# Attention scores of a whole query group in one go, z of a batch in five pieces, logits dealt out anew

## The chip, the core and the metric

One core of a Trainium2 chip runs the program. The metric is device microseconds of one execution; the kernel before takes 2508.85 us, the median of 3 runs (2508.83 to 2512.48).

## What is computed

Attention over 8 batches of 2496 rows, and then a layer of 8 experts on its result. The first part, cut to what matters here:

```python
scores = (1.0 / S) * np.matmul(z, z.transpose(0, 2, 1))   # z: 8 x 2496 x 64
attn = np.maximum(scores, 0.0) ** 2
out = np.matmul(attn, v)                                   # v: 8 x 2496 x 256
x = u * out
logits = x.reshape(B * S, D) @ w_gate                      # 256 x 8
```

The second part sorts the logits, deals every expert the same number of rows and runs two matmuls per expert. The change doesn't touch it.

## The kernel before, in words

**Tiles.** A batch has KT = 20 key tiles of 128 rows (the last holds 64) and NQ = 5 query groups of 512 columns (the last holds 448). The list `seq` walks over batches, groups and key tiles: 800 steps, called n below. Group 0 of a batch begins at step n0, and a *window* below is the 20 steps of one group. g0 to g4 are the five windows of a batch.

**What a step does.** Every product of float32 is made from a high and a low half in float32r. `scores` (L1003 to L1017) makes the scores of two key tiles at a time, each with 64 rows of the PE array, so that two matmuls run side by side; three rounds (high·high, high·low, low·high) per pair. Each result, a PSUM tile `sc` of 128x512, is rectified and scaled into SBUF as `r` by `rectify` (L1019), on ACT (L1025) or "aside" on DVE (L1023). There are SCB = 6 tiles `sc`, in rotation, so the first tile of pair j waits for the release of tile 2j-6 and the second for that of tile 2j-5. Then ACT squares `r` in place (L1029), ACT or DVE makes the high half `hi` (`split_hi`, L1036 or L1038), DVE the low half `lo` (`split_lo`, L1047), and `av` multiplies with the halves of v: six matmuls of 128 rows (L1060, L1062, L1063) into two PSUM banks.

**Goes.** Scores aren't made step by step but GO = 10 key tiles at a time: a *go* is five pairs in a row. After the first 24 tiles (six goes of four) the goes begin at tile 24, 34, ... 794: 78 goes. A go runs LA = 4 steps before its first tile is used, so that four steps of `av` lie between the end of a go and the use of its first tile.

**Order.** From step 20 on the order on PE, ACT and DVE is the program's order, written out by hand. In a step n: the go that is due; what `first_in` holds; the squares and halves of step n+4; `av(n)`; what `todo` holds. So DVE has a go's asides first, and behind them the logits that were put at the same step.

**After a group.** At the end of a window `take_acc` copies the two banks to SBUF (DVE L1069 "the take", ACT L1071). PE turns them back two steps into the next window (`turn_back`, L1083), DVE multiplies with u (`post_mul`, L1094). Then follow 32 logits of the group: one DVE instruction over 128x256 for each of 4 row tiles and 8 experts (`post_logits`, L1111), which `logits_at` deals out: some with the go in the middle of the next window, some with the go that begins the window after it, some between. Only the logits of the batch's last row tile have 64 rows.

**z and v of the next batch.** `z_turn` transposes z of the next batch piece by piece (L955, two transposes), ACT and DVE split it (`z_whole`, L962 and L963), and eight DMAs on SP's queue put the halves into place. ZH and ZL are one tile of 2560 columns per batch, with two buffers. The five pieces of a batch are turned ten steps apart, over the windows g1 to g3. In g4 one v tile per step is split for the next batch (`split_v`, ACT L994, DVE L995). In g1 `settle` (some twelve short DVE instructions) finds the best expert of the previous batch's rows.

Of the kernel before, what the change touches and what calls it, by code (L numbers as in the profile page):

```python
# [8 lines left out]
F32 = mybir.dt.float32  # L9
F32R = mybir.dt.float32r  # L10
# [4 lines left out]
AF = mybir.ActivationFunctionType  # L15
# [838 lines left out]
def attention(tc, u, v, z, w_gate, xd, identf, made, first, scale):  # L854
    nc = tc.nc
    B, S, D = u.shape
    DQ = z.shape[-1]
    lg, m = first["lg"], first["m"]
    E = lg.shape[2]
    NT = S // 128  # L860
    TL = S - NT * 128
    KT = NT + 1
    DH = D // 128
    NQ = KT // 4
    J = B * NT + B // 2
    JP = lg.shape[1]
    LA = 4
    RING = KT + 2
    SCB = 6
    GO = KT // 2  # L870
    with ExitStack() as ctx:
        io = ctx.enter_context(tc.tile_pool(name="io", bufs=3))
        zp = ctx.enter_context(tc.tile_pool(name="zp", bufs=2))
# [42 lines left out]
            return src[b, :NT * 128].rearrange("(p i) d -> p i d", i=NT)  # L916

        def load(src, b, g, name, width, copies):
            t = io.tile([128, 4, width], F32, name=name, bufs=2 if width == DQ else 3)
            n = min(4, NT - 4 * g)  # L920
            nc.sync.dma_start(t[:, :n], rows(src, b)[:, 4 * g:4 * g + n])
            if n < 4:
                for c in range(copies):
                    nc.sync.dma_start(t[c * TL:(c + 1) * TL, n], src[b, NT * 128:])
            return t
# [14 lines left out]
            UR[b, g] = load(u, b, g, "ur", D, 2)  # L940

        def z_turn(b, g):
            if g == 0:
                ZH[b] = zp.tile([128, KT * 128], F32R, name="zh")
                ZL[b] = zp.tile([128, KT * 128], F32R, name="zl")
            p = ps.tile([128, 512], F32, name="sc", bufs=SCB)
            c = slice(512 * g, 512 * g + 512)
            t = ZI.pop((b, g))
            if (b, g) == (0, 0):
                for i in range(4):  # L950
                    nc.tensor.transpose(p[:, i * 128:i * 128 + 128], t[:, i].rearrange("p s d -> p (s d)"), identf)
                return (nc.scalar.activation(ZH[b][:, c], p, AF.Copy),
                        nc.vector.tensor_sub(ZL[b][:, c], p, ZH[b][:, c].bitcast(F32)))
            for i in range(2):
                nc.tensor.transpose(p[:, i * 128:i * 128 + 128],  # L955
                                    t[:, 2 * i:2 * i + 2].rearrange("p s d -> p (s d)"), identf)
            ZT[b, g] = p

        def z_whole(b, g):
            p = ZT.pop((b, g))[:, :256]  # L960
            h, l = [io.tile([128, 256], F32R, name=name, bufs=1) for name in ("zsh", "zsl")]
            nc.scalar.activation(h, p, AF.Copy)  # L962
            nc.vector.tensor_sub(l, p, h.bitcast(F32))  # L963
            for t, src in ((ZH, h), (ZL, l)):
                v4 = t[b][:, 512 * g:512 * g + 512].bitcast(F32).rearrange("p (i s q) -> p i s q", s=2, q=128)
                v3 = src.bitcast(F32).rearrange("p (i q) -> p i q", q=128)
                for s in range(2):
                    for half in range(2):
                        nc.sync.dma_start(v4[DQ * half:DQ * half + DQ, :, s], v3[DQ * s:DQ * s + DQ])

        def z_parts(b, g):
            c = slice(512 * g, 512 * g + 512)
            p = ZT.pop((b, g))
            zh, zl = [t[b][:, c].rearrange("p (i s q) -> p i s q", s=2, q=128) for t in (ZH, ZL)]
            src = p[:, :256].rearrange("p (i q) -> p i q", q=128)
            for s in range(2):
                r = slice(DQ * s, DQ * s + DQ)
                nc.scalar.activation(zh[r, :, s], src[r], AF.Copy)
            for s in range(2):
                r = slice(DQ * s, DQ * s + DQ)  # L980
                nc.vector.tensor_sub(zl[r, :, s], src[r], zh[r, :, s].bitcast(F32))

        def swap_z(b, c):
            for t in (ZH, ZL):
                v4 = t[b][:, c].bitcast(F32).rearrange("p (m s q) -> p m s q", s=2, q=128)
                nc.sync.dma_start(v4[:DQ, :, 1], v4[DQ:, :, 1])
                nc.sync.dma_start(v4[DQ:, :, 0], v4[:DQ, :, 0])

# [14 lines left out]
        def scores(lo, hi):  # L1003
            for n in range(lo, hi, 2):
                b, g, kt = seq[n]
                w = width(g)
                q = slice(g * 512, g * 512 + w)
                pair = [ps.tile([128, 512], F32, name="sc", bufs=SCB)[:, :w] for _ in range(2)]
                for key, query in ((ZH, ZH), (ZH, ZL), (ZL, ZH)):
                    for s in range(2):  # L1010
                        r = slice(DQ * s, DQ * s + DQ)
                        k = (kt + s) * 128
                        nc.tensor.matmul(pair[s], key[b][r, k:k + 128], query[b][r, q],  # L1013
                                         start=key is ZH and query is ZH, stop=key is ZL)
                for s in range(2):
                    SC[n + s] = pair[s]
                    rectify(n + s, n + s == lo + 1)  # L1017

        def rectify(n, aside):  # L1019
            p = SC.pop(n)  # L1020
# [9 lines left out]

        def split_hi(n):
            h = wk.tile([128, 512], F32R, name="hi", bufs=LA + 1)[:, :width(seq[n][1])]
            b, g, _ = seq[n]
            here = (0, 3, 5, 8) if g == NQ - 1 and b < B - 1 else (0, 4, 8)
            if n >= KT and ((n - LA) % GO not in here or n == B * NQ * KT - 2):
                nc.scalar.activation(h, R[n], AF.Copy)  # L1036
            else:
                nc.vector.tensor_copy(h, R[n])  # L1038
            HI[n] = h
# [148 lines left out]
        def at(n, f, *a):  # L1188
            todo.setdefault(n, []).append((f, a))

        def logits_at(m0):
            if m0 + KT < B * NQ * KT:
                g = m0 // KT - 1
                mid, more, end, rest = {NQ - 4: (14, 4, 14, 0), NQ - 3: (16, 6, 10, 0),
                                        NQ - 2: (8, 0, 14, 10)}.get(g % NQ, (14, 0, 14, 4))
                return ([m0 + GO] * mid + [m0 + GO + 3 + i for i in range(more)] + [m0 + KT] * end
                        + [m0 + KT + 4 + i % 6 for i in range(rest)])
            return [m0 + 4 + i // 2 for i in range(12)] + [m0 + GO] * 9 + [m0 + GO + 1 + i // 2 for i in range(11)]

        for c in range(0, (B - 1) * NT // 16 * 16, 16):  # L1200
            at((B * NQ - 1) * KT + 2 + c // 16, premask, c, c + 16)
        for b in range(B - 1):
            at(((b + 1) * NQ + 1) * KT + 12, settle, b * NT, (b + 1) * NT)
        for b in range(B):
            for g in range(NQ):
                n0 = (b * NQ + g) * KT
                m0 = n0 + KT
                if m0 == B * NQ * KT:
                    at(m0 - 6, turn_u, b, g)
                    at(m0 - 1, last_mul, b, g)  # L1210
                else:
                    for d in range(2):
                        at(m0 - 1, take_acc, b, g, d)
                    at(m0 + 2, turn_back, b, g)
                    for d in range(2):
                        at(m0 + 3, post_mul, b, g, d)
                for e, n in enumerate(logits_at(m0) if m0 < B * NQ * KT else ()):
                    first_in.setdefault(n, []).append((post_logits, (b, g, e // E, e % E)))
                if b or g:
                    at(n0 - 3, load_u, b, g)  # L1220
            n0 = b * NQ * KT
            if b == B - 1:
                at(B * NQ * KT + 1, last_logits, b, NQ - 1)
                at(B * NQ * KT + 2, settle, b * NT + 4 * (NQ - 1), J)
                at(B * NQ * KT + 3, last_rows, b, NQ - 1)
            if b:
                for g in range(NQ):
                    m = n0 + GO * (g - 2 * NQ + 2) + 5
                    at(m - 9, load_z, b, g)
                    at(m, z_turn, b, g)  # L1230
                    at(m + 1, z_whole, b, g)
                    at(n0 - KT + 4 * g - 8, load_v, b, g)
                for kt in range(KT):
                    at(n0 - KT + kt, split_v, b, kt)
            else:
                for kt in range(KT):
                    at(kt - 4, split_v, 0, kt)
                for g in range(1, NQ):
                    t = 4 * g - LA - 3
                    at(t, z_turn, 0, g)  # L1240
                    at(t + 1, z_parts, 0, g)
                    at(t + 2, swap_z, 0, slice(512 * g, 512 * g + 512))
                    if g >= 3:
                        at(4 * g - 13, load_z, 0, g)
                        at(4 * g - 11, load_v, 0, g)
# [70 lines left out]
```

## Time and profile before

| | |
|---|---|
| median of 3 runs | 2508.85 us |
| the profiled execution | 2515.77 us |
| its span, first to last instruction | 2514.0 us |
| granted TensorE clock, mean | 0.997 |
| attention, first to last score matmul | 5.9 to 1412.5 us |
| PE busy | 2472.2 us, 98% of the span |
| DVE busy | 2068.5 us, 82% |
| ACT busy | 1494.5 us, 59% |

The attention's 1.4 ms is the stretch that the change touches; the expert layer follows it. Matmuls are pipelined: a matmul of 512 columns has a duration of 0.39 us in the profile, and the next begins 0.23 us after it. So a change on PE is read from the distances between starts, not from busy time.

### The profile page before, as it was taken

The numbers are of one execution on the slowest core, as the hardware profiler recorded it, in microseconds if no ns is written. First come the engines' busy times: TensorE is split into PE (matmuls) and PEld (weight loads), VectorE is DVE, ScalarE is ACT, GpSimd is POOL, SyncE is SP. The second block draws the span as 40 slices with busy tenths as digits, with TensorE's granted clock in tenths as the row PEclk, the third lists the DMA queues.
The fourth block names the chain that finished last, engine by engine and source line by source line (L and its number), as shares of the span: only waits on it lengthen the run. The fifth ranks groups of instructions, "written<-read, shape, count | busy, mean of one in ns | idle before, by whom it ended". The sixth has DMA issues, their size and how long they took to land.

```text
span 2514.0 us, 43326 instructions
## 1 busy us (share of the span) xinstructions
PE 2472.2 (98%) x15350; PEld 2042.1 (81%) x15350; DVE 2068.5 (82%) x6370; ACT 1494.5 (59%) x2939; POOL 361.2 (14%) x508
## 2 busy tenths in 40 slices
PE   9999999999999999999999999999999999999997
PEld 6787888888888888878888878788888888888886
DVE  8888898898898898898888887979696969696332
ACT  7787887888787887878877522323232323233332
POOL 3000000000000000000000013233333333333332
PEclk9999999999999999999999999999999999999999
DMA  4222221221222112222110011212121212122110
GB/s 146 73 70 61 63 72 51 69 75 39 66 75 66 51 63 72 67 64 50 59 33 26 17 52 41 67 46 70 46 68 48 70 45 73 43 92 63 42 46 33
DMA packets 93721, 149.23 MB, mean 59 GB/s; under 512 B 16192, under 2 KB 61632, under 8 KB 93504
## 3 DMA queue, kind: packets, MB, share of 16 engines
q1 hardware_dynamic: 78272, 105.03, 14.2%
q0 software_dynamic: 15232, 41.44, 5.2%
q8 instruction: 120, 1.97, 0.3%
q14 instruction: 97, 0.79, 0.1%
HBM read 86.12 MB, written 40.89 MB: 51 GB/s over the span
## 4 chain that ended last, share of the span: by engine, by line
PE 88%; DVE 7%; issue 3%; ACT 1%; POOL 1%; DMA 0%; POOLq 0%; ACTq 0%; DVEq 0%; SPq 0%
PE acc L1060 14%; PE acc L1063 14%; PE acc L1062 13%; PE sc L1013 11%; PE y L748 10%; PE hp L652 5%; PE hp L653 5%; PE y L750 5%; PE hp L654 5%; PE srch L281 1%; PE sc L1083 1%; PE srch L529 1%; DVE mask L124 1%; DVE ob L523 1%; PE xp L325 1%
## 5 line engine op out<-in xcount | busy, mean ns | idle before, releaser
L1060 PE MATMUL acc<-hi,vh 128*128 128x512 f32 (+1 forms) x1600 | 631.7, 395 | 2.4 <-ACT vh L994 1.3
L1063 PE MATMUL acc<-hi,vl 128*128 128x512 f32 (+1 forms) x1600 | 616.2, 385 | 0.0
L1047 DVE TENSOR_TENSOR lo<-r,hi 128x512 fp32r<-128x512 f32 (+1 forms) x760 | 510.7, 677 | 117.1 <-ACT hi L1036 104.8
L1062 PE MATMUL acc<-lo,vh 128*128 128x512 f32 (+1 forms) x1520 | 586.4, 386 | 0.2 <-DVE lo L1047 0.2
L730 ACT ACTIVATE hh<-hp 128x512 fp32r<-128x512 f32 (+1 forms) x319 | 187.3, 587 | 592.0 <-PE hp L654 478.2
L1029 ACT ACTIVATE r<-r 128x512 f32<-128x512 f32 (+1 forms) x800 | 487.5, 651 | 1.7 <-DVE r L1023 1.5
L1111 DVE SCALAR_TENSOR_TENSOR lt<-xs,wgb 128x256 bf16<-128x256 f32 x1248 | 451.8, 421 | 1.0
L748 PE MATMUL y<-w,hh 128*128 128x512 f32 x1216 | 447.5, 400 | 2.4 <-DVE y L773 1.7
L1036 ACT ACTIVATE hi<-r 128x512 fp32r<-128x512 f32 (+1 forms) x533 | 342.9, 643 | 167.9 <-issue 111.9
L1025 ACT ACTIVATE r<-sc 128x512 f32<-128x512 f32 (+1 forms) x716 | 361.9, 609 | 94.4 <-PE sc L1013 87.6
L1060 PEld LDWEIGHTS acc<-hi,vh 128*128 128x128 f32 x1600 | 300.4, 188 | 83.2 <-issue 28.5
L1063 PEld LDWEIGHTS acc<-hi,vl 128*128 128x128 f32 x1600 | 300.3, 188 | 56.3
L1062 PEld LDWEIGHTS acc<-lo,vh 128*128 128x128 f32 x1520 | 285.7, 188 | 48.5 <-DVE lo L1047 0.5
L748 PEld LDWEIGHTS y<-w,hh 128*128 128x128 f32 x1216 | 228.2, 188 | 51.6 <-DVE y L773 3.0
L652 PE MATMUL hp<-xh,w1h 128*128 128x512 f32 (+2 forms) x642 | 256.7, 400 | 2.1 <-DVE hl__31174 L732 1.3
L590 POOL DMA_INDIRECT xg<-xd,idx x160 | 176.8, 1105 | 545.7 <-issue 245.1
L653 PE MATMUL hp<-xl,w1h 128*128 128x512 f32 (+2 forms) x642 | 251.0, 391 | 0.1
L654 PE MATMUL hp<-xh,w1l 128*128 128x512 f32 (+2 forms) x642 | 249.1, 388 | 0.0
L256 POOL IOTA slot<- 128x256 bf16 x1 | 1.5, 1532 | 1392.0 <-PE sc L1121 1392.0
L781 POOL DMA_INDIRECT out_dram<-y,idx x160 | 162.3, 1014 | 195.7 <-DVE y L773 111.1
L1013 PE MATMUL sc<-zh 64*128 64x512 f32 (+1 forms) x800 | 179.7, 416 | 4.9 <-DVE r L1023 4.2
L1013 PE MATMUL sc<-zl,zh 64*128 64x512 f32 (+1 forms) x800 | 169.6, 386 | 0.0
(1197 smaller groups left out, 3601.0 us busy)
## 6 DMA issues: line engine op xcount, KB each, us to landing
vr<-in_v_dram SPq DMA_DIRECT2D x32, 512.0 KB, 3.7
ur<-in_u_dram SPq DMA_DIRECT2D x32, 512.0 KB, 4.8
xd<-xs SPq DMA_DIRECT2D x32, 512.0 KB, 2.9
wr<-in_moe_w_dram SPq DMA_DIRECT2D x32, 512.0 KB, 5.4
zh<-zsh SPq DMA_DIRECT2D x140, 64.0 KB, 2.1
zl<-zsl SPq DMA_DIRECT2D x140, 64.0 KB, 2.0
zin<-in_z_dram SPq DMA_DIRECT2D x31, 128.0 KB, 2.2
vr<-in_v_dram SPq DMA_DIRECT2D x8, 384.0 KB, 3.3
```

The source lines that it names most:

```text
L652: nc.tensor.matmul(p[:, c], wh, xh, start=(d == 0), stop=False)
L653: nc.tensor.matmul(p[:, c], wh, xl, start=False, stop=False)
L654: latest["mm"] = nc.tensor.matmul(p[:, c], wl, xh, start=False, stop=(d == DH - 1))
L748: nc.tensor.matmul(o, h[:, c], w.rearrange("p s d -> p (s d)"), start=(f == 0), stop=(f == FT - 1), skip_group_check=True)
L1013: nc.tensor.matmul(pair[s], key[b][r, k:k + 128], query[b][r, q], start=key is ZH and query is ZH, stop=key is ZL)
L1025: recent["r"] = nc.scalar.activation(r, p, AF.Relu, scale=scale)
L1029: nc.scalar.activation(R[n], R[n], AF.Square)
L1047: recent["l"] = nc.vector.tensor_sub(l, a, h.bitcast(F32))
L1060: nc.tensor.matmul(o, vh, h, start=(kt == 0), stop=False)
L1062: nc.tensor.matmul(o, vh, l, start=False, stop=False)
L1063: nc.tensor.matmul(o, vl, h, start=False, stop=last)
L1111: nc.vector.scalar_tensor_tensor(t[r], XS[b, g][r, i], 1.0, WG["rows"][r, e], op0=OP.mult, op1=OP.mult, accum_out=lg[r, j, e:e + 1])
```

## The change

GO becomes 20: the goes begin at tile 24, 44, ... 784, 39 of them, one at the start of every window. Of a go's 20 tiles four (numbers 3, 6, 9 and 12) are rectified aside on DVE, where it was one of ten. DVE makes `hi` in five steps of a window (3 in 10 before, 4 in 10 in g4). Every batch has z in five pieces of 512 columns, and only piece 0 has two buffers; so pieces 1 to 4 of the next batch can be written only after the go that begins g4, and their turns move into g4 (steps 3, 7, 11 and 15), that of piece 0 to step 12 of g3. u has two buffers in place of three, `r` (whose count is GO + 3) 23 in place of 13. The logits: of most groups 18 between the steps of the next window and 14 with the go after it; those of g3 are dealt 6, 14 and 12, those of g4 12, 14 and 6, the last number standing for the window after that go. So DVE has these logits, before and after:

| window | before | after |
|---|---|---|
| g0 | 14 + 10 + 14 = 38 | 14 + 12 + 12 = 38 |
| g1 | 14 + 4 + 14 = 32 | 14 + 6 + 18 = 38 |
| g2 | 14 + 4 + 14 + 4 = 36 | 14 + 18 = 32 |
| g3 | 14 + 16 + 6 = 36 | 14 + 18 = 32 |
| g4 | 10 + 8 = 18 | 14 + 6 = 20 |

In the last window of all, `premask` of the first 128 rows' columns stands with the go instead of one call per step, and eight of the go's logits are moved ahead into the window before.

```diff
-    GO = KT // 2
+    GO = KT
+    HALF = GO // 2
+    ASIDE = (3, 6, 9, 12)
+    HERE = (2, 6, 10, 14, 18)
...
-            t = io.tile([128, 4, width], F32, name=name, bufs=2 if width == DQ else 3)
+            t = io.tile([128, 4, width], F32, name=name, bufs=3 if name == "vr" else 2)
...
         def z_turn(b, g):
-            if g == 0:
-                ZH[b] = zp.tile([128, KT * 128], F32R, name="zh")
-                ZL[b] = zp.tile([128, KT * 128], F32R, name="zl")
+            for part, name in ((ZH, "zh"), (ZL, "zl")):
+                part[b, g] = zp.tile([128, 512], F32R, name=f"{name}{g}", bufs=1 if g else 2)
...
                         r = slice(DQ * s, DQ * s + DQ)
-                        k = (kt + s) * 128
-                        nc.tensor.matmul(pair[s], key[b][r, k:k + 128], query[b][r, q],
+                        p, c = divmod(kt + s, 4)
+                        nc.tensor.matmul(pair[s], key[b, p][r, c * 128:c * 128 + 128], query[b, g][r, :w],
                                          start=key is ZH and query is ZH, stop=key is ZL)
                 for s in range(2):
                     SC[n + s] = pair[s]
-                    rectify(n + s, n + s == lo + 1)
+                    rectify(n + s, n + s == lo + 1 if hi - lo < HALF else n + s - lo in ASIDE)
...
         def split_hi(n):
-            b, g, _ = seq[n]
-            here = (0, 3, 5, 8) if g == NQ - 1 and b < B - 1 else (0, 4, 8)
-            if n >= KT and ((n - LA) % GO not in here or n == B * NQ * KT - 2):
+            if n >= KT and ((n - LA) % GO not in HERE or n == B * NQ * KT - 2):
...
         def logits_at(m0):
             if m0 + KT < B * NQ * KT:
-                g = m0 // KT - 1
-                mid, more, end, rest = {NQ - 4: (14, 4, 14, 0), NQ - 3: (16, 6, 10, 0),
-                                        NQ - 2: (8, 0, 14, 10)}.get(g % NQ, (14, 0, 14, 4))
-                return ([m0 + GO] * mid + [m0 + GO + 3 + i for i in range(more)] + [m0 + KT] * end
-                        + [m0 + KT + 4 + i % 6 for i in range(rest)])
-            return [m0 + 4 + i // 2 for i in range(12)] + [m0 + GO] * 9 + [m0 + GO + 1 + i // 2 for i in range(11)]
+                n = m0 // KT - 1
+                own, go, late = {NQ - 2: (6, 14, 12), NQ - 1: (12, 14, 6)}.get(n % NQ, (18, 14, 0))
+                if n == B * NQ - 3:
+                    own, go = own + go - 6, 6
+                return ([m0 + 4 + i * 16 // own for i in range(own)] + [m0 + KT] * go
+                        + [m0 + KT + 5 + i * 15 // max(late, 1) for i in range(late)])
+            return [m0 + 4 + i // 2 for i in range(4 * E)]
...
-            at((B * NQ - 1) * KT + 2 + c // 16, premask, c, c + 16)
+            first_in.setdefault((B * NQ - 1) * KT, []).append((premask, (c, c + 16)))
...
-                    m = n0 + GO * (g - 2 * NQ + 2) + 5
-                    at(m - 9, load_z, b, g)
+                    m = n0 - KT + (3, 7, 11, 15)[g - 1] if g else n0 -KT - 8
+                    at(m - 6, load_z, b, g)
                     at(m, z_turn, b, g)
                     at(m + 1, z_whole, b, g)
```

## Rows read from the trace of the kernel before

**Rows 1.** The page, part 1: busy time, share and instructions of each engine.

```profile
PE 2472.2 (98%) x15350; PEld 2042.1 (81%) x15350; DVE 2068.5 (82%) x6370; ACT 1494.5 (59%) x2939; POOL 361.2 (14%) x508
```

**Rows 2.** The waits, 100 to 1380 us: who waited for whom, us, times, longest.

```profile
PEld acc L1060 <- issue: 25.4, 72, 0.4
PEld sc L1013 <- issue: 25.1, 73, 0.4
...
PE sc L1013 <- DVE r L1023: 4.2, 7, 0.7
```

**Rows 3.** The timeline of PE around one go: start, us, instruction.

```profile
457.85 0.39 PE L1063 MATMUL acc<-hi,vl 128*128 128x512 f32 x1
458.17 0.50 PE L1013 MATMUL sc<-zh 64*128 64x512 f32 x2
...
458.97 0.39 PE L1013 MATMUL sc<-zh 64*128 64x512 f32 x2
...
460.79 0.41 PE L1013 MATMUL sc<-zh,zl 64*128 64x512 f32 x2
...
462.46 0.39 PE L1063 MATMUL acc<-hi,vl 128*128 128x512 f32 x1
```

**Rows 4.** Busy time by window: length, then PE, PEld, DVE, ACT, POOL, clock, DMA.

```profile
439.44:475.50 36.06, 36.06 (x191) 29.02 (x190) 31.83 (x106) 28.84 (x56) 0.00 (x0) 1.00 0.26 66
...
511.28:543.49 32.21, 32.21 (x187) 28.64 (x187) 29.17 (x86) 29.74 (x70) 0.00 (x0) 1.00 0.30 91
543.49:580.12 36.63, 36.00 (x188) 28.53 (x187) 32.94 (x113) 29.06 (x56) 0.00 (x0) 1.00 0.15 49
...
403.91:439.97 36.06, 36.06 (x192) 28.96 (x190) 32.92 (x111) 28.85 (x55) 0.00 (x0) 1.00 0.23 62
511.68:545.08 33.40, 33.40 (x200) 29.57 (x198) 30.33 (x89) 31.02 (x72) 0.00 (x0) 1.00 0.30 95
...
580.64:616.71 36.07, 36.07 (x192) 28.96 (x191) 32.21 (x111) 28.83 (x55) 0.00 (x0) 1.00 0.23 61
```

**Rows 5.** The timeline of DVE in one g1, whose go begins at 403.38.

```profile
404.51 0.68 DVE L1023 TENSOR_SCALAR r<-sc 128x512 f32<-128x512 f32 x1
405.11 0.42 DVE L1111 SCALAR_TENSOR_TENSOR lt<-xs,wgb 128x256 bf16<-128x256 f32 x1
...
410.18 0.43 DVE L1038 CAST hi<-r 128x512 fp32r<-128x512 f32 x1
...
412.24 0.69 DVE L1047 TENSOR_TENSOR lo<-r,hi 128x512 fp32r<-128x512 f32 x1 [0.30 <-ACT hi L1036]
...
423.14 0.69 DVE L1023 TENSOR_SCALAR r<-sc 128x512 f32<-128x512 f32 x1 [0.77 <-PE sc L1013]
...
439.36 0.69 DVE L1047 TENSOR_TENSOR lo<-r,hi 128x512 fp32r<-128x512 f32 x1 [0.55 <-ACT hi L1036]
```

**Rows 6.** The timeline of DVE in one g4 and at the go behind it.

```profile
516.89 0.40 DVE L1038 CAST hi<-r 128x448 fp32r<-128x448 f32 x1 [0.54 <-ACT r L1029]
...
536.61 0.63 DVE L1047 TENSOR_TENSOR lo<-r,hi 128x448 fp32r<-128x448 f32 x1 [0.28 <-ACT hi L1036]
...
545.08 0.62 DVE L1069 COPY at<-acc 128x448 f32<-128x448 f32 x1
...
545.95 0.68 DVE L1023 TENSOR_SCALAR r<-sc 128x512 f32<-128x512 f32 x1
```

**Rows 7.** The timeline of PE in the same go, which begins at 543.49.

```profile
545.67 0.39 PE L1013 MATMUL sc<-zh 64*128 64x512 f32 x1
546.69 0.50 PE L1013 MATMUL sc<-zh 64*128 64x512 f32 x1 [0.63 <-DVE r L1023]
```

**Rows 8.** The timeline of ACT in the go that begins at 403.38.

```profile
404.38 4.72 ACT L1025 ACTIVATE r<-sc 128x512 f32<-128x512 f32 x9 [0.63 <-PE sc L1013]
408.91 1.73 ACT L1029 ACTIVATE r<-r 128x512 f32<-128x512 f32 x3
```

**Rows 9.** The timeline of PE around one turn of z, which lies between these.

```profile
416.09 0.40 PE L1063 MATMUL acc<-hi,vl 128*128 128x512 f32 x1
...
417.01 0.39 PE L1063 MATMUL acc<-hi,vl 128*128 128x512 f32 x1
```

More of the change, by code (lines that the diff above doesn't have):

```diff
@@ L942, in z_turn @@
         def z_turn(b, g):
-            if g == 0:
-                ZH[b] = zp.tile([128, KT * 128], F32R, name="zh")
-                ZL[b] = zp.tile([128, KT * 128], F32R, name="zl")
+            for part, name in ((ZH, "zh"), (ZL, "zl")):
+                part[b, g] = zp.tile([128, 512], F32R, name=f"{name}{g}", bufs=1 if g else 2)
             p = ps.tile([128, 512], F32, name="sc", bufs=SCB)
-            c = slice(512 * g, 512 * g + 512)
             t = ZI.pop((b, g))
@@ L951, in z_turn @@
                     nc.tensor.transpose(p[:, i * 128:i * 128 + 128], t[:, i].rearrange("p s d -> p (s d)"), identf)
-                return (nc.scalar.activation(ZH[b][:, c], p, AF.Copy),
-                        nc.vector.tensor_sub(ZL[b][:, c], p, ZH[b][:, c].bitcast(F32)))
+                return (nc.scalar.activation(ZH[b, g], p, AF.Copy),
+                        nc.vector.tensor_sub(ZL[b, g], p, ZH[b, g].bitcast(F32)))
             for i in range(2):
@@ L964, in z_whole @@
             for t, src in ((ZH, h), (ZL, l)):
-                v4 = t[b][:, 512 * g:512 * g + 512].bitcast(F32).rearrange("p (i s q) -> p i s q", s=2, q=128)
+                v4 = t[b, g].bitcast(F32).rearrange("p (i s q) -> p i s q", s=2, q=128)
                 v3 = src.bitcast(F32).rearrange("p (i q) -> p i q", q=128)
@@ L971, in z_parts @@
         def z_parts(b, g):
-            c = slice(512 * g, 512 * g + 512)
             p = ZT.pop((b, g))
-            zh, zl = [t[b][:, c].rearrange("p (i s q) -> p i s q", s=2, q=128) for t in (ZH, ZL)]
+            zh, zl = [t[b, g].rearrange("p (i s q) -> p i s q", s=2, q=128) for t in (ZH, ZL)]
             src = p[:, :256].rearrange("p (i q) -> p i q", q=128)
@@ L981, in z_parts, with swap_z @@
                 nc.vector.tensor_sub(zl[r, :, s], src[r], zh[r, :, s].bitcast(F32))
-        def swap_z(b, c):
+        def swap_z(b, g):
             for t in (ZH, ZL):
-                v4 = t[b][:, c].bitcast(F32).rearrange("p (m s q) -> p m s q", s=2, q=128)
+                v4 = t[b, g].bitcast(F32).rearrange("p (m s q) -> p m s q", s=2, q=128)
                 nc.sync.dma_start(v4[:DQ, :, 1], v4[DQ:, :, 1])
@@ L1006, in scores @@
                 w = width(g)
-                q = slice(g * 512, g * 512 + w)
                 pair = [ps.tile([128, 512], F32, name="sc", bufs=SCB)[:, :w] for _ in range(2)]
@@ L1241, in attention @@
                     at(t + 1, z_parts, 0, g)
-                    at(t + 2, swap_z, 0, slice(512 * g, 512 * g + 512))
+                    at(t + 2, swap_z, 0, g)
                     if g >= 3:
```

## The prediction

> **What bounds the kernel now.** First the page: PE is busy for 98% of the span, DVE for 82%, ACT for 59% [rows 1]. Then the waits in the attention: PE almost never waits for another engine there; only seven times for an `r` of DVE, 4.2 us in all. But its weight loads stop for about 0.35 us in front of nearly every go and again in front of nearly every return to `av`, and nothing that the profile shows releases them [rows 2]. So the timeline of PE around a go: inside it the starts are 0.2275 us apart (eight starts in 460.79 - 458.97). From the last `av` before the go to the third after it are 18 starts; at that pace they would take 4.10 us, and they take 4.61 [rows 3]. **A go costs 0.51 us beside its matmuls.** Last the windows: 36.06 us for g2, 32.21 for g4, 36.63 for g0 [rows 4]. PE sets all of them, but in g0 something is added. A turn of z costs PE 0.24 (0.92 for three starts [rows 9], less 0.68), and g2 has two of them, g0 none: g0 ought to last 35.58 and is 1.05 longer. Rows 7 show why: in its first go pair 3 can start only its first matmul, and the second, which needs tile 1's buffer, comes 1.02 us later, released by DVE; there DVE's take starts at 545.08, 1.6 us after the go, and the aside ends at 546.63 [rows 6]. On time the take starts 0.53 us after the go (403.91 against 403.38 [rows 4, 5]).
>
> **What is removed.** 78 goes become 39: 39 x 0.51 = 19.9 us. The stall in g0 of seven batches, 7 x 1.05 = 7.3, goes too in its present form (tile 1 is no longer DVE's). Together 27.2 us, the most that the change can give. The turns of z stay five per batch, their DMAs eight per piece; only four come to lie in g4.
>
> **The go of 20 tiles on ACT.** The first pair is ready 1.00 us after the go begins (404.38 - 403.38), each later one 3 x 0.2275 = 0.68 after the one before; ACT takes a tile every 0.503 ((408.91 - 404.38) / 9), the last of nine lasting 0.70 [rows 8]. Pair 3 starts at 2.18 [rows 7], pair 5 at 3.54, pair 9 at 6.28; a release reaches PE 0.06 after the end of the instruction (546.69 - 546.63). Sixteen tiles are ACT's. Tile 5, the fifth, is free at 1.00 + 4 x 0.503 + 0.70 + 0.06 = 3.77, 0.23 after pair 5 wants it; tile 13, the tenth, at 6.29, in time. No go before has this order. The ends are 0 (the goes of ten show no stall of this kind beyond their 0.51) and 0.23; I take the middle, 0.1. Where a window is set by DVE (next part) such a stall gives DVE as much time, so it counts in the other 25 of 39: 2.5 us.
>
> **The go on DVE.** Asides stand ahead of the logits, and DVE takes its instructions in order: in the second go of g1 it waits 0.77 us with 14 logits behind [rows 5]. Tiles 3, 6, 9 and 12 belong to pairs 1, 3, 4 and 6, ready at 1.68, 3.05, 3.73 and 5.10. A rectify takes 0.60 (405.11 - 404.51). So DVE waits 0.55, 0.77, 0.08 and 0.77 us: 2.2 in a go where it is on time, and 2.0 in g4 by the same sum with 448 columns. In exchange its waits for ACT's `hi` behind a go come half as often; I leave one of 0.30 per window [rows 5].
>
> **DVE in g1.** It is busy for 32.92 us of 36.06 where the previous batch is an odd one, and its six listed waits (0.30 first, 0.55 last) make 2.49 [rows 4, 5]; the 0.65 left is gaps that count as occupied, 33.57 in all. The change adds two rectifies (1.20) and six logits at 0.36 ((410.18 - 405.11) / 14), 2.16; it takes away one cast (0.43) and two z subtractions, priced as logits, of the same 128x256 (0.72). That is 35.8, with the waits 2.2 and 0.3 **38.3 us**. PE needs 36.06 - 0.51 - 2 x 0.24 = 35.1. DVE comes 3.2 late to the go of g2. Where the previous batch is even it is busy 0.71 less [rows 4] and 2.5 late. What that costs PE: tile 3 is free 0.53 + 0.60 + 0.69 + 0.06 = 1.88 us after the go plus the lateness, and pair 4 wants its buffer at 2.86. So 0.98 is free, and PE stalls 2.2 (three batches) or 1.5 (four): 3 x 2.2 + 4 x 1.5 = **12.6 us**. The first batch has neither the six late logits nor a `settle` here.
>
> **DVE in g4.** From take to take it takes 33.40, with waits of 2.72 (six, 0.54 first and 0.28 last [rows 6]): 30.7 occupied. Two rectifies of 448 columns (0.60 x 448/512 = 0.53 each) add 1.05, two logits 0.72, four z subtractions 1.44; three casts less save 1.15. With waits of 2.0 and 0.3 that is 35.0 us. PE needs 32.21 - 0.51 + 4 x 0.24 = 32.7 [rows 4]. DVE is 2.3 late at the go of g0. There 0.87 lie between take and rectify (a v split stands between [rows 6]), so 0.7 is free and PE stalls 1.6: 7 x 1.6 = **11.2 us**. In g2 and g3 DVE has four logits fewer than before and fits; in g0 it has as many, two rectifies more, one cast less, and the go's stall gives it the time.
>
> **What costs nothing.** ACT loses two rectifies per window and gains one `hi` (three in g4). u's two buffers: a load waits for a product that is done 14 steps earlier. z's pieces are written behind the last go that reads the old ones; the last is split in step 16 of g4, and its first reader is pair 6 of the next go, three steps and six pairs later; load_z, the eight copies and load_v keep their order on SP. `premask` and 32 logits fall into a last window that has no v to split. Without that cover a late piece would stall PE in the go of g0, where it waits for DVE anyway.
>
> **Sum.** 27.2 - 2.5 - 12.6 - 11.2 = 0.9 us gained. The profiled execution's 2515.77 becomes 2514.9; it lies 6.9 above the median of the runs, and I carry the difference over: **2508 us**. A measurement of this kernel tells some 0.2%, 5 us, from no change.
>
> **Rivals.** (1) *DVE keeps up.* The lateness is a small difference of large sums, and a window's 38.3 against 35.1 would be undone by 3 us of error: if the waits in the go overlap the lateness, or DVE starts g1 and g4 ahead. For it: the goes are seldom stalled today, with DVE at 32 of 36 us. Against: its reserve there is 3 us, and 3 us of work and waits are added to g1. Then 27.2 less up to 4 for the goes is left, 2482 to 2486; with half of the lateness the stalls come to some 6.5, and 2491 is left. Chance 0.25.
>
> (2) *The goes are paced by their evacuation, and the kernel is slower.* Place: the six `sc` buffers. PE finishes a tile every 0.34 us, ACT needs 0.503, and 16 x 0.503 = 8.05 us of copies face 30 x 0.2275 = 6.83 of matmuls. Only the last six tiles may be left over, and tile 13 comes out just in time above; ACT's reserve is the 0.63 it idles before a go [rows 8]. If every go loses 0.5 more than figured, 25 x 0.5 = 12.5 us are lost: 2520. It decides from 0.2 per go on. For it: no go so far is longer than five pairs. Against: ACT idles 7 us in most windows [rows 4]. Chance 0.18. The Trainium skill has a rule that speaks for this one (TensorEngine Tiling (Array Packing), PSUM Bottleneck): tiling makes TensorE faster but not the emptying of PSUM, whose copies may become the bottleneck; ScalarE and VectorE should share them. By the rule the longer of the two, 8.05, would set the go, 1.2 us more in each of 39, some 48 us; by the rows only what the six buffers can't hold counts, so next to nothing.
>
> (3) *ACT comes last in g4.* It is busy 31.02 of 33.40 there [rows 4]; one more tile at some 0.44 and four z copies at no more than that make 32.9, beside 0.6 of waiting at the go, and PE's time on the same count is 33.9. If ACT is 2.3 late, it adds 0.7 to DVE's 1.6, seven times: 2513. Chance 0.12.
>
> **How the numbers follow.** The forecast has 0.45: 2501 to 2514, of which 0.13 lie under 2503.8 and 0.03 over 2513.9. Faster: 0.13 + 0.25 = 0.38. Slower: 0.03 + 0.18 + 0.04 of (3) = 0.25. Within 0.2%: 0.37. The range, 2487 to 2520, leaves out the best of (1) and the worst of (2).
>
> **What would show it.** 39 goes of 30 starts, a window of g2 or g3 at some 35.1 to 35.2 us; PE waiting for DVE's `r` in the go of g0 and of g2, by 1 to 2 us each, and nowhere else; DVE waiting three or four times in a go. If the go of g2 shows no stall, the account of g1 is wrong; if g2 and g3 are longer than 35.5, the go is; if ACT has no idle time in front of g0's go, (3) holds.

## The result and the profile after

The changed kernel takes **2544.09 us** (median of four runs, 2539.55 to 2546.16) against 2509.21 us of the kernel before (four runs): a ratio of **1.0134, interval [1.0116, 1.0151]**. It is slower, where no change was forecast. The profiled execution took 2546.16 us, with a span of 2544.1. One execution of run 2 below was in a slow state (4869 us) and is left out of its ratio.

The page's first part after, to be held against [rows 1]: the busy times of PE, DVE and ACT have hardly moved, and PE's share has fallen.

```profile
PE 2474.9 (97%) x15350; PEld 2069.9 (81%) x15350; DVE 2093.8 (82%) x6395; ACT 1489.7 (59%) x2914; POOL 361.5 (14%) x508
```

Windows after, from go to go, as in [rows 4]: g4 of batch 1 (batches count from 0), then g0 to g3 of batch 2, and last a stretch inside that g4. The columns are the stretch, its length, then busy time and count of PE, PEld, DVE, ACT and POOL, TensorE's granted clock, the DMA engines' share and GB/s.

```profile
338.29:376.30 38.01, 34.58 (x196) 30.90 (x195) 29.16 (x87) 31.68 (x76) 0.00 (x0) 0.96 0.39 93
376.30:413.17 36.87, 35.68 (x188) 28.88 (x188) 35.35 (x119) 28.43 (x54) 0.00 (x0) 1.00 0.33 104
413.17:448.37 35.20, 35.20 (x187) 29.34 (x186) 32.61 (x111) 27.97 (x53) 0.00 (x0) 1.00 0.09 31
448.37:485.26 36.89, 35.48 (x187) 28.68 (x187) 33.24 (x106) 28.11 (x53) 0.00 (x0) 1.00 0.09 29
485.26:520.52 35.26, 35.26 (x189) 29.34 (x189) 30.91 (x98) 27.72 (x54) 0.00 (x0) 1.00 0.18 50
...
371.00:374.40 3.40, 3.40 (x11) 3.00 (x10) 0.48 (x1) 1.60 (x4) 0.00 (x0) 0.53 0.41 82
```

In the batch shown g0 to g3 are within half a microsecond of the prediction's working. **g4 is not:** 38.01 us where PE needs 32.7, and PE is not even busy in it (34.58 of 38.01). The seven windows of this kind take 37.56 to 39.93 us, 38.14 on average: 5.4 us too long each, 38 us in all seven.

Who waits, from the waits after, 100 to 1380 us (us in all, times, longest us); [rows 2] are the same view before:

```profile
PEld sc L956 <- DMA zin<-in_z_dram: 27.6, 14, 4.6
PE sc L956 <- DMA zin<-in_z_dram: 23.5, 11, 4.2
ACT zsh L963 <- DMA zh<-zsh: 32.1, 13, 3.9
DVE zsl L964 <- DMA zl<-zsl: 24.3, 11, 4.8
PE sc L1012 <- DVE r L1022: 9.2, 9, 1.5
PEld acc L1057 <- issue: 12.1, 35, 0.4
PEld sc L1012 <- issue: 9.9, 28, 0.4
```

The last two lines are the gain that was forecast: the stops of the weight loads that nothing shown releases have halved or more, at the return (25.4 us in 72 before) and ahead of a go (25.1 us in 73). The first four are new, and all belong to z's pieces: PE waits for the load of a piece, ACT and DVE wait until the copies out of the single staging tiles `zsh` and `zsl` have landed. What stands behind these loads and copies is shown by SP's queue in that g4 (start, length and count of the issues):

```profile
351.28 0.33 SPq L924 DMA_DIRECT2D zin<-in_z_dram  x1
352.70 1.25 SPq L970 DMA_DIRECT2D zh<-zsh  x2
354.04 0.54 SPq L1095 DMA_DIRECT2D xd<-xs  x1
354.63 1.27 SPq L970 DMA_DIRECT2D zh<-zsh  x2
356.00 2.54 SPq L970 DMA_DIRECT2D zl<-zsl  x4
358.59 0.59 SPq L924 DMA_DIRECT2D vr<-in_v_dram  x1
359.28 2.54 SPq L970 DMA_DIRECT2D zh<-zsh  x4
361.93 2.85 SPq L970 DMA_DIRECT2D zl<-zsl  x4
364.84 0.58 SPq L924 DMA_DIRECT2D vr<-in_v_dram  x1
365.47 1.16 SPq L927 DMA_DIRECT2D vr<-in_v_dram  x2
366.73 0.53 SPq L924 DMA_DIRECT2D zin<-in_z_dram  x1
367.31 1.10 SPq L927 DMA_DIRECT2D zin<-in_z_dram  x2
368.51 2.62 SPq L970 DMA_DIRECT2D zh<-zsh  x4
371.22 3.22 SPq L970 DMA_DIRECT2D zl<-zsl  x4
374.49 0.59 SPq L924 DMA_DIRECT2D ur<-in_u_dram  x1
375.18 2.55 SPq L970 DMA_DIRECT2D zh<-zsh  x4
```

From 352.70 on SP issues with hardly a pause to the end of the window. A copy takes it 0.605 us (median of 280), a piece has eight, 4.84 us, and with the loads of v, u and z between them it needs more: from the first copy of one piece to that of the next (352.70, 359.28, 368.51, 375.18) pass 6.6, 9.2 and 6.7 us. PE turns a piece every four steps, 5.1 us. So the pieces fall behind, and the load of the last one, which the code puts six steps ahead of its turn, is issued only at 366.73, behind the copies of the second piece. PE's last product of `av` stands at 365.93; the turn waits:

```profile
365.93 0.36 PE L1060 MATMUL acc<-hi,vl 128*128 128x448 f32 x1
369.49 0.33 PE L956 MATMUL sc<-identf,zin 128*128 128x128 f32 x1 [3.20 <-DMA zin<-in_z_dram]
370.05 0.30 PE L956 MATMUL sc<-identf,zin 128*128 128x128 f32 x1 [0.23 <-DMA zin<-in_z_dram]
...
371.98 0.57 PE L1059 MATMUL acc<-lo,vh 128*128 128x448 f32 x1
372.35 0.57 PE L1060 MATMUL acc<-hi,vl 128*128 128x448 f32 x1
```

Idle time is not all: after it the products start 0.37 us apart instead of 0.20, from 371.23 to 374.59, and the granted clock of 371.00 to 374.40 is 0.53: nearly all of it at 1.2 GHz, the lower of TensorE's two levels. Until 365.93 PE had been busy at the full clock (2.4 GHz), then it stood idle, and it had run again for 1.7 us when the clock fell. Nine starts at 0.37 for 0.20 are 1.5 us. With 3.4 us of waiting that makes 4.9 of the 5.3 us that this window lost.

### The profile page after: what moved, and what is told of

Same layout as the page of the kernel before. It is cut to its first block, busy times and chain, and to the rows that moved or that the text cites. A ratio compares the mean times of both kernels' runs of the same rounds, so it can differ in the third digit from the quotient of the medians.

```text
span 2544.1 us, 43329 instructions
## 1 busy us (share of the span) xinstructions
PE 2474.9 (97%) x15350; PEld 2069.9 (81%) x15350; DVE 2093.8 (82%) x6395; ACT 1489.7 (59%) x2914; POOL 361.5 (14%) x508
## 5 line engine op out<-in xcount | busy, mean ns | idle before, releaser
L1033 ACT ACTIVATE hi<-r 128x512 fp32r<-128x512 f32 (+1 forms) x586 | 372.1, 635 | 211.9 <-issue 147.4
L1108 DVE SCALAR_TENSOR_TENSOR lt<-xs,wgb 128x256 bf16<-128x256 f32 x1248 | 475.2, 419 | 2.2
L1024 ACT ACTIVATE r<-sc 128x512 f32<-128x512 f32 (+1 forms) x638 | 313.9, 613 | 46.5 <-PE sc L1012 45.7
L1012 PE MATMUL sc<-zh,zl 64*128 64x512 f32 (+1 forms) x800 | 197.4, 386 | 0.5 <-DMA zl<-zsl 0.4
L1012 PE MATMUL sc<-zl,zh 64*128 64x512 f32 (+1 forms) x800 | 197.1, 387 | 0.0
```

The costliest lines, as they stand in the source:

```text
L1012: nc.tensor.matmul(pair[s], key[b, p][r, c * 128:c * 128 + 128], query[b, g][r, :w], start=key is ZH and query is ZH, stop=key is ZL)
L1108: nc.vector.scalar_tensor_tensor(t[r], XS[b, g][r, i], 1.0, WG["rows"][r, e], op0=OP.mult, op1=OP.mult, accum_out=lg[r, j, e:e + 1])
```

## The experiments

Ratios are to the kernel before, timed beside it on the same chip (its medians were 2509 to 2517 us). The trace of a run is of one execution. In the expectations A is the theory that z's crowded place in g4 costs the time, B one that does without it, and D the rival that holds the DMA engines' load responsible. The later ones say what they mean by S and T.

**1. Only z's place, in the kernel before.** Goes of ten, z in one tile, logits as they were.

```
-                    m = n0 + GO * (g - 2 * NQ + 2) + 5
-                    at(m - 9, load_z, b, g)
+                    m = n0 - KT + (3, 7, 11, 15)[g - 1] if g else n0 - KT - 8
+                    at(m - 6, load_z, b, g)
```

> The kernel before (goes of 10, z with two buffers) with one edit: the turns and loads of z stand where the change puts them (piece 0 in g3, pieces 1 to 4 in g4 at steps 3, 7, 11 and 15). Theory A (SP issues the eight z copies of a piece in 8 x 0.605 = 4.8 us, with the loads some 6 us per piece, while PE gives it only 5.1 us between two turns in g4): the loss comes with the place of the turns alone, 2535 to 2550 us, PE waiting for zin in g4 and the clock at half behind it. Theory B (the go of 20 tiles, or the evacuation, makes it slow): no loss here, 2507 to 2513.

Measured: 2560.64 us, 1.0176 [1.0159, 1.0193], 43 us over before and above A's range. The move alone costs more than the whole change: z's crowded place is enough for a loss of this size, and the rest of the change is worth something. But the loss falls in another place than A had it. No turn waits for `zin`; most of it is in the first ten-tile half of g0, which takes 22.3 to 25.6 us in place of 19.5. There PE waits for ACT's `r` (13.1 us in all, seven times), while ACT and DVE wait for the staging tiles (24.3 and 19.2 us).

**2. The loads of z earlier** (four buffers of `zin`; to make room, one of `r` less).

```
-                    at(m - 6, load_z, b, g)
+                    at(n0 - 2 * KT + 4 * g, load_z, b, g)
```

> The changed kernel with the five loads of z moved ahead into g2 and g3 (four zin buffers; r has one buffer less, 22, to make room). Theory A (SP's issue time for the copies is the bound): PE no longer waits for zin, but the copies still follow one another at some 5 us per piece, so ACT and DVE wait for zsh and zsl and the last pieces land at the go of g0: only a part comes back, 2515 to 2532. Theory C (only the load of the last piece stands too late in SP's order): the whole loss of 5.4 us per g4 comes back, 2544 - 38 = 2506, at most 2510.

Measured: 1.0087 [1.0067, 1.0107]. The wait for `zin` is gone and g4 takes some 32.7 to 33.8 us, but the go behind it lasts 11.7 to 16 us in place of 7.6: the wait has moved on, to the split of the last piece: in the go of g0 PE waits in every batch for the `sc` tile that DVE's `zsl` frees (7.9 us in all). By the ratios some 12 us came back, by the attention's own time (the table below run 12) 6.7.

**3. The copies of zl on POOL's queue.**

```
-                        nc.sync.dma_start(v4[DQ * half:DQ * half + DQ, :, s], v3[DQ * s:DQ * s + DQ])
+                        (nc.sync if t is ZH else nc.gpsimd).dma_start(v4[DQ * half:DQ * half + DQ, :, s], v3[DQ * s:DQ * s + DQ])
```

> The changed kernel with the four copies of zl of each piece issued by POOL in place of SP, which halves SP's work per piece to about 2.4 us and leaves transfers and order alone. Theory A: no wait for zin, g4 windows of 32.7 to 33.5 in place of 38.1, 2503 to 2510; if one POOL issue takes over 1.3 us the stalls stay in part. Theory D (the DMA engines are too busy in g4, their share is 0.7 there): the copies land as late as before, 2538 to 2546.

Measured: 1.0142 [1.0125, 1.0159], no gain. The wait for `zin` is all but gone (1.9 us in place of 23.5) and g4 takes 34.1 to 36.0 us, but the go of g0 now lasts 12 to 17.6: DVE waits 34.5 us in all for the staging tile, and PE 25.6 for DVE's `r` and 12.9 for `zsl`. So A was right on the turns and wrong on the time. The total alone would speak against SP's queue as a cause; runs 9 to 11 show why it had to miss.

**4. The same, with the logits of g0 dealt out anew** (fewer at the go of g2).

```
-                own, go, late = {NQ - 2: (6, 14, 12), NQ - 1: (12, 14, 6)}.get(n % NQ, (18, 14, 0))
+                own, go, late = {NQ - 2: (6, 14, 12), NQ - 1: (12, 14, 6), 0: (12, 14, 6)}.get(n % NQ, (18, 14, 0))
```

> As the run with zl on POOL, and besides the logits of g0 dealt 12, 14 and 6 in place of 18, 14 and 0, so that g1 has 32 and g2 38 of them. My account of DVE in g1 says the stall in the go of g2 (1.8 us in three batches, 0.4 in four) goes: 7 us less than the run with zl on POOL. If that stall has another cause (the 64-row logits, settle), no more than 2 us less.

Measured: 1.0138 [1.0121, 1.0155]. The windows of g2 fell to 35.2 us, so the stall there was DVE's. The medians differ by 3.2 us only, where the executions of run 3 alone differ by 6.5. Run 8 repeats it on better ground.

**5. Four DMAs per piece and no staging tile** (ACT and DVE write the halves in place, with twice the instructions).

```
-                    at(m + 1, z_whole, b, g)
+                    at(m + 1, z_parts, b, g)
+                    at(m + 2, swap_z, b, g)
```

> The changed kernel with z split straight into its pieces by ACT and DVE (two instructions each in place of one, as the first batch does it) and only the other half copied: 4 DMAs per piece in place of 8, and no staging tiles zsh and zsl. Theory A2 (a piece takes too long through one staging tile and eight issues one after the other on SP: zsh and zsl are free again only when their copies are issued and have landed): g4 falls from 38.1 to 33 to 34 us (ACT has 4 x 0.27 and DVE 4 x 0.34 us more there), 0.5 to 0.9% faster than the changed kernel. Theory D (the DMA engines are too busy): half the copies are gone too, so it gains some as well, but the loads of zin still come late. If neither, no more than 0.2%.

Measured: 1.0045 [1.0028, 1.0061], 0.9% under the changed kernel. g4 comes down to 32.7 to 33.2, while the go of g0 still lasts 10 to 13.4 us: there PE now waits for DVE's `r` (14.7 us in all). DVE has the extra instructions; that they make it late is likely, and was not tested by itself.

**6. Two buffers of each staging tile** (one of `r` less).

```
-            h, l = [io.tile([128, 256], F32R, name=name, bufs=1) for name in ("zsh", "zsl")]
+            h, l = [io.tile([128, 256], F32R, name=name, bufs=2) for name in ("zsh", "zsl")]
```

> The changed kernel with two buffers for zsh and zsl (r has 22 in place of 23). If the single staging tile is what spaces the pieces, ACT and DVE no longer wait for copies, and a third or more of the loss comes back (10 us and up). If SP's issue time of 4.8 us per piece is, next to nothing changes, since the copies only queue up later: within 5 us of the changed kernel.

Measured: 1.0094 [1.0077, 1.0111]. Now g0 takes 35.2 to 35.6 in six of seven batches, nearly without a stall (39.6 in the seventh), and g4 still 36 to 39: the turns wait for `zin` (22.4 us in all) behind SP's copies.

**7. Three pieces with two buffers, turned early; only two in g4** (one step of the ring, two buffers of `r` and the buffer of `ztwo` pay for it).

```
-                part[b, g] = zp.tile([128, 512], F32R, name=f"{name}{g}", bufs=1 if g else 2)
+                part[b, g] = zp.tile([128, 512], F32R, name=f"{name}{g}", bufs=1 if g > 2 else 2)
...
-                    m = n0 - KT + (3, 7, 11, 15)[g - 1] if g else n0 -KT - 8
-                    at(m - 6, load_z, b, g)
+                    m = n0 - KT + (4, 12)[g - 3] if g > 2 else n0 - KT - (32, 20, 8)[g]
+                    at(m - 9, load_z, b, g)
```

> The changed kernel with two buffers for z's pieces 0 to 2, turned in g3 and before (32, 20 and 8 steps before g4 ends its predecessor), and only pieces 3 and 4 in g4, at steps 4 and 12, 8 steps apart (11 us per piece). Room comes from r (21), the v ring (21) and the first z tile. Theory A: two pieces of 16 copies fit between their turns, g4 is 32.7 to 33.5 us, the stall of g0 at most 1.5: 34 us less than the changed kernel, that is -0.1% to -0.5% of the kernel before. If the go of 20 tiles itself is what costs, still over 1% slower than before.

Measured: 2501.73 us, **0.9942 [0.9925, 0.9958]**, faster than before. Its windows of g4 and the g0 behind it:

```profile
331.08:363.26 32.18, 32.18 (x191) 29.32 (x190) 30.30 (x92) 30.98 (x74) 0.00 (x0) 1.00 0.40 104
363.26:398.62 35.36, 35.36 (x187) 28.67 (x186) 33.44 (x112) 28.43 (x54) 0.00 (x0) 1.00 0.24 76
```

PE is busy in the whole of both. Copies and staging tiles are as in the changed kernel; the distance between the pieces is another, and with it the loads stand nine steps ahead of the turns in place of six.

**8. Run 7 with the logits of run 4.**

> As the run before it, with the logits of g0 dealt 12, 14 and 6. The stall in the go of g2 (1.8 us in three batches, 0.4 in four) goes: 6 to 8 us less than the run before it, 0.4 to 0.8% faster than the kernel before.

Measured: 2495.06 us, **0.9912 [0.9895, 0.9929]**, 6.7 us under run 7. g2 is at 35.4 in every batch but the last (35.2), where it was 35.4 to 35.8 in some and 37.2 in the others.

Runs 2, 3 and 6 each mended one thing and got back little or nothing. So they were put together.

**9. Runs 2 and 6 together** (early loads, two staging buffers).

> The changed kernel with both one-edit repairs together: the loads of z's pieces one go earlier (four buffers of zin) and two buffers of each staging tile zsh and zsl. Each alone gave back something (ratios to before 1.0087 and 1.0094). Theory S (SP's issue time of the copies is a bound by itself: eight at about 0.6 us, at least 5 us per piece beside the other loads, against 5.1 us between two turns): the pieces stay crowded on SP, and the last one is late; g4 and the go of g0 together still hold at least 3 us more per batch than in e7_z_two (32.2 and 35.4), so a ratio of 1.000 to 1.006. Theory T (the late load and the single staging tile are all of it): g4 32 to 33, the following g0 at most 36, so a ratio of 0.994 to 0.997.

Measured: 2523.91 us, 1.0059 [1.0042, 1.0076], as S has it. No load of z is late and no staging tile is awaited, yet the go of g0 lasts 10 to 13 us. Two of its waits (all batches together) and one of its matmuls, in a go that began at 367.81; then what SP had still to issue, with DVE's end of the last split:

```profile
PEld sc L1012 <- DMA zl<-zsl: 13.8, 12, 1.8
PE sc L1012 <- DMA zl<-zsl: 9.8, 7, 1.5
```

```profile
376.12 0.49 PE L1012 MATMUL sc<-zh,zl 64*128 64x512 f32 x1 [1.43 <-DMA zl<-zsl]
```

```profile
364.09 2.62 SPq L970 DMA_DIRECT2D zh<-zsh  x4
365.46 0.42 DVE L964 TENSOR_TENSOR zsl<-sc,zsh 128x256 fp32r<-128x256 f32 x1
366.82 2.54 SPq L970 DMA_DIRECT2D zl<-zsl  x4
369.45 2.55 SPq L970 DMA_DIRECT2D zh<-zsh  x4
372.10 2.54 SPq L970 DMA_DIRECT2D zl<-zsl  x4
```

DVE has finished the last piece's `zsl` at 365.88, ahead of the go, and SP issues the copies of the last two pieces back to back until 374.64, 6.8 us into it. The first product that needs the last copy runs at 376.12.

**10. Run 9 with the copies of zl on POOL** (the edit of run 3).

> e9_zin_staging with the copies of zl issued by POOL instead of SP, so that SP has four copies per piece (2.4 us) instead of eight. Theory S: most of what e9 still loses comes back: g4 and the following g0 within 1.5 us of e7_z_two's, a ratio of 0.994 to 0.999. Rival D (what holds the pieces is the landing of the copies on DMA engines that are loaded anyway, not their issue): no better than e9 within 0.2%.

Measured: 2495.97 us, **0.9946 [0.9929, 0.9962]**: the same edit that gave nothing in run 3 is worth 28 us, 1.1%, here (20.6 of them in the attention), and all five pieces stay where the change put them. Windows of g4 and g0, which answer to the first two shown above:

```profile
330.94:363.56 32.62, 32.62 (x195) 29.71 (x194) 30.80 (x93) 31.58 (x76) 8.46 (x15) 1.00 0.53 132
363.56:400.02 36.46, 35.74 (x188) 28.87 (x187) 33.65 (x113) 28.65 (x54) 0.88 (x2) 1.00 0.28 84
```

The DMA engines' load is not what held run 9: their share in g4 is higher here than in any other g4 shown (0.53), and a copy takes twice as long to land as in run 9. The list of issues (count, KB each, median us to landing), run 9 and then run 10:

```profile
zh<-zsh SPq DMA_DIRECT2D x140, 64.0 KB, 2.1
zl<-zsl SPq DMA_DIRECT2D x140, 64.0 KB, 2.1
```

```profile
zh<-zsh SPq DMA_DIRECT2D x140, 64.0 KB, 4.4
zl<-zsl POOLq DMA_DIRECT2D x140, 64.0 KB, 4.4
```

So D falls. The Trainium skill says of this (Trainium Kernel Development and Optimization, Key Constraints) that DMAs of SP, ACT and POOL share the same 16 engines, and that issuing from several only saves the sequencer's issue time. The runs agree, landings being slower; here that "only" is some 21 us of the attention.

**11. Run 10 with single staging tiles again.**

> e10_zin_staging_pool with the staging tiles zsh and zsl single again (loads of z one go earlier, copies of zl on POOL). e3_zl_pool, which had the loads late and single staging, gave 1.0142. If the single staging tile is a bound of its own beside SP (a piece then waits until the copies of the piece before have landed: 2.4 us of issue and 2.1 us of landing behind two casts, some 6 to 7.5 us per piece against 5.1 between two turns), three turns run late by 1 to 2.4 us each: 3 to 7 us per batch, a ratio of 1.003 to 1.015. If with the early loads the staging is no bound: a ratio within 0.2% of e10's.

Measured: 2545.5 us, 1.0129 [1.0104, 1.0154]. The single tile is a bound of its own, and through it the time of landing counts. POOL's issues and the DVE subtractions that fill `zsl`, in one g4:

```profile
354.89 2.32 POOL L970 DMA_DIRECT2D zl<-zsl  x4 [21.57 <-DVE zsl L964]
364.51 2.33 POOL L970 DMA_DIRECT2D zl<-zsl  x4 [7.30 <-DVE zsl L964]
```

```profile
363.79 0.42 DVE L964 TENSOR_TENSOR zsl<-sc,zsh 128x256 fp32r<-128x256 f32 x1 [4.94 <-DMA zl<-zsl]
370.42 0.42 DVE L964 TENSOR_TENSOR zsl<-sc,zsh 128x256 fp32r<-128x256 f32 x1 [1.60 <-DMA zl<-zsl]
375.92 0.42 DVE L964 TENSOR_TENSOR zsl<-sc,zsh 128x256 fp32r<-128x256 f32 x1 [0.52 <-ACT at L1068]
```

POOL has issued the first piece's copies by 357.21, and DVE gets the tile back only at 363.79, 6.6 us later. DVE takes its work in order, so its other tasks stand still too, and PE is short of `r` in the go of g0 (25.4 us of waits for it, 9.2 in the changed kernel).

**12. Run 10 with the logits of run 4.**

> e10_zin_staging_pool with the logits of g0 dealt out as those of g4 are (12 in its own steps, 14 at the go, 6 late), so that DVE is not late in the go of g2. In the run with the pieces of z moved the same edit gave 6.7 us. Here the goes of g2 that follow an odd batch lose 1.7 us (three times) and the others 0.3: a gain of 5 to 7 us, a ratio of 0.991 to 0.993. If POOL's issues of the copies now push something else late, less than 3 us.

Measured: 2487.73 us against 2510.64 of before, **0.9910 [0.9894, 0.9927]**, by the ratios some 9 us under run 10, a little more than expected, and no different from run 8. Runs 7, 8, 10 and 12 beat both kernels.

**The three edits together** (L early loads, G second staging buffer, P zl on POOL; G with P was not tried):

| edits | ratio to before | attention, us |
|---|---|---|
| none (the change) | 1.0134 | 1410.3 |
| L | 1.0087 | 1403.6 |
| G | 1.0094 | 1402.0 |
| P | 1.0142 | 1428.9 |
| L, G | 1.0059 | 1389.8 |
| L, P | 1.0129 | 1421.6 |
| L, G, P | **0.9946** | 1369.2 |

The last column is the time from the go at tile 24 to the last product of `av`, in the one execution that was profiled (1380.8 before, 1363.2 in run 7); executions of one run differ by 1 to 14 us, the one of 4869 aside. It leaves out the rest of the program, and there P does something that no expectation had: in the five runs where POOL issues copies the program ends 3.6 us after the last scatter of the result, in the seven other runs and in both kernels 9.5 us. SP's last waits, run 9 and then run 10:

```profile
SPq L1310 <- PEq L1310: 7.3, 2, 6.8
```

```profile
SPq L1310 <- PEq L1310: 1.6, 2, 1.1
```

Why is not shown. So 5.9 us of what the ratios of runs 10 and 12 gain belong to no piece of z, and behind run 3's ratio stands an attention 18.6 us longer than that of the change.

One chain carries each piece: load, turn, split into the staging tile, eight issues on SP, landing, staging tile free. PE asks for a piece every 5.1 us, and three links of the chain need more: the load queued behind the copies, the single tile that is held until the copies land, and SP's issues. In every run that mended one or two of them PE waited on another; L with P is even worse than L, for the copies issued by POOL hold the single tile for longer (DVE waits for it 37.2 us in run 11, 11.0 in run 2).

## Why the prediction was wrong

**The step that failed stands under "What costs nothing": "load_z, the eight copies and load_v keep their order on SP", at a price of nothing.** Their order was kept; their rate was not looked at. Before, the pieces were ten steps apart; the change puts them four apart, and no row of SP's queue had been read. Eight copies at 0.605 us with the loads beside them need 6.6 to 9.2 us against 5.1. The term was 0 and measured 7 x 5.4 = 38 us, with the half clock of TensorE in it. "Without that cover a late piece would stall PE in the go of g0, where it waits for DVE anyway" failed too: the load of a late piece stalls PE ahead of that, at the turn in g4, and the clock with it.

The other terms, each as the profile after has it:

- **39 goes removed, 0.51 us each.** Right in size: g1 takes 35.14 to 35.21 and g3 35.25 where 35.1 to 35.2 were worked out, and run 7, with the pieces spaced, is 14.6 us faster than before.
- **The evacuation of the go on ACT**, 0.1 per go: g1 lies some 0.07 over the 35.1. Rival 2, a go paced by its evacuation (8.05 us of copies in the prediction's count), falls; from the last `av` before to the first behind it a go of g1 takes 7.57 us, which is 31 starts of 0.2275 and the 0.51.
- **DVE late in g1**, a stall of 2.2 us in g2 behind an odd batch and of 1.5 behind an even one. Measured by g2 against the 35.17 of g1: 1.7 (36.89 to 36.93) and 0.3 (35.45 to 35.52). The mechanism is shown by runs 8 and 12, where fewer logits take it away; the light case was sized too high, by 1.2 us four times.
- **DVE late in g4**, 1.6 us in the go of g0, seven times. Measured 1.4 on average (36.53 less 35.17). The size agrees but in this kernel not the reason: DVE is late because its split of the last piece waits 4.52 us for the staging tile:

```profile
376.00 0.42 DVE L964 TENSOR_TENSOR zsl<-sc,zsh 128x256 fp32r<-128x256 f32 x1 [4.52 <-DMA zl<-zsl]
```

 In run 10, with all four pieces in g4 and no such wait, 1.1 us is left (36.30 less 35.17), and PE's longer stops in these goes have several releasers: copies of `zh` in three batches (0.6 to 1.05 us), ACT's `r` in one (0.5), DVE's `r` in one (0.65, elsewhere 0.1 or nothing). So the term came out by luck: how late the count of DVE's work alone would make it is not shown; run 10 leaves room for at most the 1.1.
- **PE's own need in g4**, 32.7 us: run 10, where nothing is late, takes 32.61 to 32.78.
- **Rival 3**, ACT last in g4: it falls. ACT's long waits there are for the staging tile (32.1 us), and run 10, with ACT as busy as in the change, holds 32.62.

**The sum.** Against the profiled execution the forecast was 2514.9 and the time 2546.2, 31.3 more. The terms give +38.1 for g4, -4.7 and -1.4 for the two kinds of g2 (4 x 1.18 and 3 x 0.47), -1.7 for g0: 30.3. The slower side was given to two rivals at ACT; none of the rivals was at SP. By medians the miss is 36 us (2508 against 2544.09): the profiled execution before lay 6.9 us above its median, the one after 2.1, so some 5 us of it have no term here.

What stays open: how the loss of run 1 divides among the three links was not tried, and neither was G with P. That POOL's copies and SP's beside them land at 4.4 us instead of 2.1 in run 10 (2.6 and 2.9 in run 11) is measured; why, is not.

## What to carry to other kernels

When work is moved closer together, compare the new distance with the time that each link of its chain needs, the DMA queue's issue time included: count times the length of one issue, plus everything else in that queue. A queue that is never seen to wait can be the bound, and the stalls then carry other names (a load, a staging buffer, a busy VectorE). If one mended link gives nothing, it is not acquitted: mend the others with it before it is ruled out, and compare the stretch that the edit touches, beside the total.

## What was not expected of the hardware

An issue of a 64 KB copy within SBUF occupied SP for 0.605 us and POOL for 0.59, while the copy landed after 2.1: eight copies in a row are 4.84 us of issuing, and a copy has landed 2.1 us after its issue began. With half of the copies issued by POOL the landing took 4.4 us (run 10), and yet the kernel was faster. An idle time of PE of 3.2 us was followed by 3.4 us at a granted clock of 0.53, so that the stall cost nearly half as much again. And once POOL had issued copies, the program ended 5.9 us sooner behind its last scatter.
